# Two attentions on one core: sums over keys moved to TensorE, a normalization by 32x32 transposes, and a scheduler that keeps engines free for the next scores

## The chip, the cores and the metric

One core of one Trainium2 chip. The time is device microseconds (us) of one execution. ScalarE is called ACT in the profile, TensorE PE (its weight loads PEld), VectorE DVE, GpSimd POOL. A matmul here always needs its stationary operand loaded first; "step" means the time from the start of one instruction to the start of the next on the same engine.

## The reference, cut to what matters

Two attentions over 2048 positions and 448 channels, 16 heads of 28, their results side by side.

```python
# A: 16 query heads share one key and one value head
scores = einsum("bhqd,bkd->bhqk", q, k) * Dh ** -0.5      # 16 x 2048 x 2048
o = einsum("bhqk,bkd->bhqd", softmax(scores), v)          # then @ wo
# B: every query sees W = 8 keys, at distances 0, 2, ..., 14
logits = einsum("bhsd,bhswd->bhsw", q, k[idx]) * scale    # masked before position 0
o = einsum("bhsw,bhswd->bhsd", softmax(logits), v[idx])   # then @ wo
```

A's 67 million exponentials are the bulk. B is small, and is worked off beside A.

## The kernel before

The program is straight-line code, ordered by a planner inside the kernel. Every operation is added with an engine, a planned duration in us and a priority. The planner runs the engines forward in its own time, takes on each the best ready operation, and so fixes the order of each engine's instructions. Only the order reaches the chip: there each instruction starts when its engine is free and its semaphores have come.

```python
class Sched:
    LAT = 0.13                        # planned semaphore latency
    FULL = {2: 1500.0, 3: 1200.0}     # below this activity, scores use the full array height
    ...
def t_mm(n):                          # planned duration of one matmul of n columns
    return 0.02 + 0.42e-3 * max(n, 100)          # 0.235 us for 512
```

A's loop: the scores lie in PSUM in two slots of three and two banks. TensorE fills a slot, ScalarE takes the exponential of the whole slot (1536 or 1024 columns) and frees it. In 60 of the 410 rounds the third score goes to VectorE instead, which reads it (`d_x`) and approximates the exponential; its slot is free only after both reads. Scores need 28 rows of the array. They are issued as three matmuls beside each other in 32-row tiles (planned 0.32), or, when TensorE has been little active, one after the other at full height.

```python
def qk(e):                                    # scores of one slot
    for i, (sc, t, tb, j) in enumerate(us):
        if box[0].full:                       # full height, zero-padded keys
            e.matmul(g.bank(b0 + i), g.kz[:, j, ...], g.qT[:, sc % 2, t, :], ...)
        else:                                 # 32-row tile at row 32 j
            e.matmul(g.bank(b0 + i), g.kT[32*j:32*j+32, ...], g.qT[32*j:32*j+32, ...],
                     tile_position=(32 * j, 0))
```

B's eight products per block (`prod2`) are added in pairs on VectorE (`padd`), and TensorE sums the four that remain while it transposes. A's result for four heads and 512 queries lies in one PSUM bank, each head in 32 partitions, the sum of the exponentials in row 28. It is normalized in six stages over four engines:

```python
# a_quad_end: PV -> PV_sb copy (VectorE; ScalarE for the last one)
#   -> 4 fp32 matmuls with sel4 pick the sums -> reciprocal (VectorE)
#   -> rrep broadcast (GpSimd) -> 4 matmuls with ident -> product oTn (VectorE)
```

The softmax here doesn't subtract the row's maximum and nothing guards it: scores larger than these inputs give would overflow.

## Time and profile before

| | |
|---|---|
| time, median of 3 | 479.02 us (478.52 to 479.02) |
| profiled run | 476.5 us from the first to the last instruction, clock 1.000 |
| exponentials | 410 on ScalarE, from 12.67 to 467.75 us |
| last A output issued, last B output issued | 473.54, 474.06 us |

The prediction below shows most of the profile's lines. Some more: two groups by shape (busy us and mean ns of one, then idle time of the engine before them and what ended it), and the end of the timeline (columns: start in us, length in us, engine, line, operation, what it writes and reads, count).

```profile
L748 PEld LDWEIGHTS ps<-qT,kz 128*128 128x128 bf16 x305 | 21.1, 101 | 34.7 <-ACT expT L766 25.9 <-issue 0.7 <-ACT gcol L671 0.2
L823 DVE TENSOR_SCALAR d_x<-ps 128x512 f32<-128x512 f32 x60 | 41.4, 689 | 11.3 <-PE ps L750 7.4 <-PE ps L748 2.6
```

**How lateness is counted.** Throughout, the "late sum" adds, over all pairs of exponentials with no other ScalarE instruction between, the step minus 1.330 us after a 1536-column one and minus 0.904 us after a 1024-column one. Before it is 18.4 us. Steps at least 0.06 us late are sorted by the scores that the second exponential waited for: full-height scores, row-tiled scores behind a busy TensorE, and slots that VectorE's `d_x` read released late.

### The profile page before, as it was taken

The numbers are of one execution on the slowest core, as the hardware profiler recorded it, in microseconds if no ns is written. First come the engines' busy times: TensorE is split into PE (matmuls) and PEld (weight loads), VectorE is DVE, ScalarE is ACT, GpSimd is POOL, SyncE is SP. The second block draws the span as 40 slices with busy tenths as digits, with TensorE's granted clock in tenths as the row PEclk, the third lists the DMA queues.
The fourth block names the chain that finished last, engine by engine and source line by source line (L and its number), as shares of the span: only waits on it lengthen the run. The fifth ranks groups of instructions, "written<-read, shape, count | busy, mean of one in ns | idle before, by whom it ended". The sixth has DMA issues, their size and how long they took to land.

```text
span 476.5 us, 8559 instructions
## 1 busy us (share of the span) xinstructions
PE 451.4 (95%) x3605; PEld 178.3 (37%) x3605; DVE 375.6 (79%) x614; ACT 454.6 (95%) x431; POOL 29.4 (6%) x45
## 2 busy tenths in 40 slices
PE   8999999999999999999999999989999999989896
PEld 3443333434333424333434333333343343433332
DVE  4446878988878886889868887989868988896963
ACT  3899999999999999999999999999999999999993
POOL 8100010000000000000000010010001000010100
PEclk9999999999999999999999999999999999999999
DMA  9780211020200320002200330020200330220001
GB/s 195 147 216 1 89 30 58 11 78 12 87 11 30 111 83 12 11 19 79 78 11 10 107 107 11 10 78 12 87 12 21 107 106 12 88 88 11 0 11 48
DMA packets 41717, 27.32 MB, mean 57 GB/s; under 512 B 17090, under 2 KB 41520, under 8 KB 41680
## 3 DMA queue, kind: packets, MB, share of 16 engines
q1 hardware_dynamic: 39600, 25.25, 18.4%
q10 hardware_dynamic: 1776, 0.81, 0.7%
q0 software_dynamic: 304, 0.73, 0.6%
q8 instruction: 28, 0.46, 0.4%
q14 instruction: 9, 0.07, 0.1%
HBM read 17.60 MB, written 5.52 MB: 49 GB/s over the span
## 4 chain that ended last, share of the span: by engine, by line
ACT 65%; PE 31%; SPq 1%; DMA 1%; DVE 1%; issue 0%; DVEq 0%
ACT expT L766 64%; PE ps L750 7%; PE ps L924 6%; PE ps L790 5%; PE ps L748 4%; PE ps L852 2%; PE ps L696 2%; PE ps L940 1%; SPq L560 1%; DMA xT_A<-in_A_x_dram 1%; PE ps L883 1%; PE ps L1038 1%; PE ps L660 1%; PE ps L392 1%; ACT e_t L1001 0%
## 5 line engine op out<-in xcount | busy, mean ns | idle before, releaser
L766 ACT ACTIVATE expT<-ps 128x1024 bf16<-128x1024 f32 (+1 forms) x410 | 446.1, 1196 | 7.2 <-PE ps L750 4.5
L750 PE MATMUL ps<-qT,kT 32*128 32x512 bf16 x719 | 107.9, 384 | 8.8 <-ACT expT L766 5.9
L748 PE MATMUL ps<-qT,kz 128*128 128x512 bf16 x305 | 88.1, 382 | 9.6 <-ACT expT L766 7.5
L790 PE MATMUL ps<-expT,v_aug 128*32 128x512 bf16 x964 | 95.7, 389 | 0.4
L750 PEld LDWEIGHTS ps<-qT,kT 32*128 32x128 bf16 x719 | 26.5, 90 | 73.8 <-ACT expT L766 52.3
L823 DVE TENSOR_SCALAR d_x<-ps 128x512 f32<-128x512 f32 x60 | 41.4, 689 | 11.3 <-PE ps L750 7.4
L966 DVE TENSOR_TENSOR stage<-qTB,kTB 112x1024 bf16<-112x1024 bf16 x64 | 42.8, 682 | 9.1 <-PE ps L975 9.0
L790 PEld LDWEIGHTS ps<-expT,v_aug 128*32 128x32 bf16 x964 | 24.4, 92 | 66.3 <-issue 62.3
L924 PE MATMUL ps<-xT_B,wqkv 128*112 128x512 bf16 (+1 forms) x128 | 44.6, 407 | 0.0
L860 POOL COPY rrep<-rden 128x512 bf16<-128x512 bf16 x15 | 16.8, 1122 | 393.8 <-DVE rden L858 393.8
L1020 DVE TENSOR_TENSOR prod<-Vsh,a_n 128x896 bf16<-128x896 bf16 x64 | 38.4, 624 | 1.3 <-PE ps L1031 1.3
L830 DVE SCALAR_TENSOR_TENSOR d_u<-d_x 128x1024 f32<-128x1024 uint16 x30 | 36.5, 1217 | 0.1
L834 DVE SCALAR_TENSOR_TENSOR dexp<-d_u,d_x 128x1024 int16<-128x1024 f32 x30 | 36.4, 1214 | 0.1
L832 DVE SCALAR_TENSOR_TENSOR d_u<-d_u,d_x 128x1024 f32<-128x1024 f32 x30 | 36.3, 1211 | 0.1
L748 PEld LDWEIGHTS ps<-qT,kz 128*128 128x128 bf16 x305 | 21.1, 101 | 34.7 <-ACT expT L766 25.9
L1031 PE MATMUL ps<-ident,prod 128*112 128x128 bf16 x256 | 25.6, 226 | 0.0
L975 PEld LDWEIGHTS ps<-ones,stage 112*128 112x128 bf16 x512 | 20.5, 96 | 12.7 <-issue 7.0
L975 PE MATMUL ps<-ones,stage 112*128 112x4 bf16 x512 | 24.3, 167 | 0.0
L1031 PEld LDWEIGHTS ps<-ident,prod 128*112 128x112 bf16 x256 | 19.3, 129 | 12.1 <-issue 8.6
L924 PEld LDWEIGHTS ps<-xT_B,wqkv 128*112 128x112 bf16 (+1 forms) x128 | 14.1, 126 | 20.7 <-issue 17.4
L852 PEld LDWEIGHTS ps<-sel,PV_sb 128*128 128x128 f32 x128 | 18.9, 190 | 5.7 <-issue 4.1
L696 PE MATMUL ps<-xT_A,wq 128*128 128x512 bf16 x64 | 20.5, 384 | 0.5 <-DVE v_aug L675 0.3
(107 smaller groups left out, 383.0 us busy)
## 6 DMA issues: line engine op xcount, KB each, us to landing
Vsh<-v_scratch SPq DMA_DIRECT2D x16, 896.0 KB, 4.6
v_scratch<-Vst SPq DMA_DIRECT2D x16, 112.0 KB, 1.7
out_dram<-outB SPq DMA_DIRECT2D x16, 112.0 KB, 1.7
out_dram<-outA SPq DMA_DIRECT2D x14, 112.0 KB, 1.7
wqkv<-in_B_wqkv_dram SPq DMA_DIRECT2D x1, 672.0 KB, 5.0
stage<-in_A_x_dram ACTq DMA_DIRECT2D x1, 448.0 KB, 3.4
wo_B<-in_B_wo_dram SPq DMA_DIRECT2D x4, 98.0 KB
wo<-in_A_wo_dram SPq DMA_DIRECT2D x4, 98.0 KB
```

Source lines behind the costliest of these rows:

```text
L748: r = e.matmul(g.bank(b0 + i), g.kz[:, j, 128 * tb:128 * tb + 128], g.qT[:, sc % 2, t, :], start=True, stop=True)
L750: r = e.matmul(g.bank(b0 + i), g.kT[32 * j:32 * j + 32, 128 * tb:128 * tb + 128], g.qT[32 * j:32 * j + 32, sc % 2, t, :], start=True, stop ...
L766: x = a("act", t_exp(w), lambda e, b0=b0, w=w, n=n: e.activation(g.expT[:, n % ERING, 0:w], g.ps[:, 512 * b0:512 * b0 + w], ACT.Exp, scale ...
L790: x = e.matmul(g.bank(PVBANK, p0=32 * j, p1=32 * j + 32), g.v_aug[:, w, tb, :], src, start=first, stop=last, tile_position=(0, 32 * j))
L823: a("dve", t_dve_ps(512), lambda e: e.tensor_scalar(out=xx[:, 512 * h:512 * h + 512], in0=g.bank(bank), scalar1=-128.0 * A2, scalar2=128.0 ...
L830: a("dve", t_dve_1x(1024), lambda e: e.scalar_tensor_tensor(out=u, in0=lo, scalar=EP * F, in1=lo, op0=ALU.add, op1=ALU.mult), R=di, W=["d_ ...
L834: a("dve", t_dve_1x(1024), lambda e: e.scalar_tensor_tensor(out=out, in0=v, scalar=EL / F ** 3, in1=xx, op0=ALU.mult, op1=ALU.subtract), R ...
L924: a("pe", t_mm(512), lambda e, u=u, t=t, kt=kt, w=w: e.matmul(g.bank(u.bank, p1=KC), g.wqkv[64 * (kt // 3):, kt, w * D + KC * t:w * D + KC ...
L966: op = a("dve", t_dve_2x(1024), lambda e, t=t, qv=qv, kv=kv: e.tensor_tensor(out=g.prodT[0:KC, t, :, :], in0=qv, in1=kv, op=ALU.mult), R=R ...
L975: r = e.matmul(g.bank(u.bank, 128).rearrange("p (h w) -> p h w", w=WIN)[:, 4 * t:4 * t + 4, w], g.prodT[0:KC, t, w, :], g.ones4[:, :], sta ...
L1020: a("dve", t_dve_2x(2 * D), lambda e, qr=qr, Vv=Vv, av=av: e.tensor_tensor(out=g.prod2[:, 2 * qr:2 * qr + 2, :].rearrange("p w (d h) -> p ...
L1031: a("pe", 0.09, lambda e, u=u, t=t, w=w: e.matmul(g.bank(u.bank, 128, 128 * t, p1=KC), g.padd[:, w, KC * t:KC * t + KC], g.ident[:, :], st ...
```

## The change

Its intent: take B's pair additions off VectorE, replace the six-stage normalization by four VectorE instructions, and let the planner refuse work on TensorE and VectorE that would run into the next scores or the next `d_x` read. Offloaded scores now join the ordinary PV groups (PV: the product of the exponentials with the values) two passes over both slots later (`LATE`). B is released earlier. The core of the diff:

```diff
+            limit = None
+            H = tE["act"] + sum(o.dur for (_, o) in cand["act"] if o.ring)   # when ScalarE runs dry
+            if e == "dve":
+                ...
+                    limit = max(r1, H + (0.9 if n < 1 else 0) - self.QKT - 2 * self.LAT - 0.69)
+            if e == "pe":
+                ...
+                    limit = max(rq, H - self.QKT - self.LAT)
...
+                    if limit is not None and not o.ring and T + o.dur > limit + self.EPS:
+                        nxt = limit if nxt is None else min(nxt, max(limit, T + 0.02))
+                        continue
...
-                elif (o.full and area(T) < self.FULL[o.full]
+                elif (o.full and area(T) < (self.FULL[o.full] if T + 0.03 + 0.216 * o.full + self.LAT <= H + self.EPS else self.LOW)
```
```diff
     # a_quad_end
-    PV_sb copy, 4 matmuls with sel4, reciprocal, rrep on GpSimd, 4 matmuls with ident, product   # (abridged)
+            a("dve", t_dve_ps(w), lambda e, cs=cs: e.transpose(out=g.PV_T[:, t % 2, cs], in_=g.bank(PVBANK)[:, cs]), ...)
+            a("dve", 0.25, lambda e, pt=pt, bs=bs: e.reciprocal(out=g.rden[:, t % 2, bs], in_=pt[:, bs, DH]), ...)
+            a("dve", t_dve_1x(w), ... product with rden broadcast over 32, to oN ...)
+            a("dve", 0.12 + 1.04e-3 * w, ... e.transpose(out=g.oTn[:, t, cs], in_=oN) ...)
     # b_out
-        for hf in range(2): padd = prod2[hf] + prod2[hf + 2]      # VectorE (abridged)
-            for w in range(4): matmul(padd[:, w], ident)
+            for w in range(WIN): matmul(prod2[:, w], ident)       # WIN = 8
-    B0 = 32.0
-    BSTEP = 24.5
+    B0 = 30.0
+    BSTEP = 23.6
```

## The prediction

> **What bounds the kernel now.** I read four views in this order: the page's busy table and chain, the groups by shape, the instructions at ScalarE's late starts, and the end of the timeline.
>
> ```profile
> PE   451.4 (95%) x3605; PEld 178.3 (37%) x3605; DVE 375.6 (79%) x614; ACT 454.6 (95%) x431; POOL 29.4 (6%) x45
> PEclk9999999999999999999999999999999999999999
> ACT 65%; PE 31%; SPq 1%; DMA 1%; DVE 1%; issue 0%; DVEq 0%
> L766 ACT ACTIVATE expT<-ps 128x1024 bf16<-128x1024 f32 x264 | 264.9, 1047 | 2.7 <-PE ps L750 2.0 <-PE ps L748 0.4
> L766 ACT ACTIVATE expT<-ps 128x1536 bf16<-128x1536 f32 x145 | 213.3, 1471 | 4.5 <-PE ps L750 2.5 <-PE ps L748 1.4
> ```
>
> ScalarE and TensorE both show 95%. ScalarE's is real work: 410 exponentials in one row from 12.67 to about 467.7 us. TensorE's contains filler (L369, L392) and full-height scores (L748) that are issued to keep its clock up. The 31% of PE in the chain is not 31% of the end: the chain goes back through the producer of each exponential, and as long as that producer ended in time it cost nothing. So the question is when it was late. The idle column before the exponentials says 7.2 us, but it understates the loss. Consecutive activations overlap by some 0.1 us, so a start that is 0.1 us late shows no idle time. I therefore took, from the trace's instruction starts, the step from each exponential to the next one. Undelayed (the 5th percentile) it is 1.330 us after a 1536-wide one and 0.904 us after a 1024-wide one. The sum of what lies above these is 18.4 us: 1.0 us after the 1536-wide and 17.4 us after the 1024-wide. The asymmetry has a reason: after a 1024-wide exponential the next slot's three score matmuls have only 0.9 us to be refilled.
>
> Of the 18.4 us, 15.8 us are in 75 steps of 60 ns or more. I sorted these by the score group in front:
> - 38 steps, 7.0 us: three full-height scores. They need 0.844 to 0.858 us from the first to the exponential, and at best start 0.055 us after the slot is released, together 0.91 us: more than 0.904 less the overlap, so even on time they cost some 0.11 to 0.2 us each.
> - 26 steps, 6.8 us: row-tiled scores (0.437 us) that found TensorE occupied. In front of them stood mostly B's projections L924 (3.8 us) and the fp32 sums L852 (1.8 us).
> - 11 steps, 2.0 us: the slot was released late by VectorE's read of an offloaded score (d_x).
>
> ```profile
> 54.52 1.13 PE L924 MATMUL ps<-xT_B,wqkv 128*112 128x512 bf16 x3
> 55.58 0.39 PE L750 MATMUL ps<-qT,kT 32*128 32x512 bf16 x3
> 56.02 2.02 ACT L766 ACTIVATE expT<-ps 128x1024 bf16<-128x1024 f32 x2 [0.58 <-PE ps L750]
> ...
> 467.99 0.40 PE L790 MATMUL ps<-expT,v_aug 128*32 128x512 bf16 x4
> 468.44 0.60 ACT L844 ACTIVATE PV_sb<-ps 128x512 f32<-128x512 f32 x1 [0.69 <-PE ps L790]
> 469.09 1.05 PE L852 MATMUL ps<-sel,PV_sb 128*128 128x4 f32 x8
> 470.19 0.26 DVE L858 RECIPROCAL rden<-ps 128x16 bf16<-128x16 f32 x1 [7.86 <-PE ps L852]
> 470.48 0.43 DVE L860 COPY rrep<-rden 128x512 bf16<-128x512 bf16 x1
> 470.96 0.40 PE L866 MATMUL ps<-ident,rrep 128*128 128x128 bf16 x4 [0.36 <-DVE rrep L860]
> 471.42 0.74 DVE L871 TENSOR_TENSOR oTn<-PV_sb,ps 128x256 bf16<-128x256 f32 x2
> ```
>
> Above the dots is one late start: the slot was free at about 54.5 us, but three projections were in front, and ScalarE idled 0.58 us. Below them is the exposed end: from the last PV (about 468.4) to the second half of oTn (472.16) 3.77 us, 3.4 us to the first half.
>
> **What the Trainium skill says.** (1) "VectorE: DVE Perf Modes", The three transpose paths: VectorE transposes in 32x32 blocks only. That suits here, since PV holds each head in one block of 32 partitions. It gives 311 ns for 128 columns of bf16; no transpose is in this trace. (2) The same page, The perf-mode tier table: a PSUM or fp32 operand holds tensor_tensor at one element a cycle. The trace agrees: 512 columns from PSUM take 0.68 to 0.69 us, 128x896 in bf16 only 0.62. (3) "TensorE: Matmul & The Clock Gate", Part 1: the clock halves when the array is too little active over windows of some 3.4 us. The trace shows 1.00 in every stretch, so nothing here tells how far activity may fall. (4) "ScalarE: Activation LUTs", What ACT_TABLE_LOAD costs: 186 ns + 0.833 ns an element, back to back some 93 ns less, so 946 ns at 1024. The trace's undelayed 904 ns is shorter and is what I use.
>
> **The change part by part.**
>
> B's sums. 32 additions on VectorE go (32 x 0.657, 20.4 us busy). TensorE sums eight products where it summed four: 256 more matmuls at 87 ns (mean step from one L1031 to the next instruction) = +22.3 us.
>
> Normalization. TensorE loses 128 fp32 instructions at a step of 118 ns (15.2 us) and 64 broadcasts at 121 ns (7.7 us), together -22.9 us. TensorE is thus unchanged in sum (-0.6), but what it gains is in pieces of 0.09 us that fit between scores, and what it loses stood in front of late scores. VectorE loses the PV copies (10.2), reciprocals (4.1), products (10.3 + 0.7) and one rrep copy (0.4): -25.7 us. It gains for each of 16 quads: transpose of 512 fp32 columns from PSUM, estimated 0.69 as other PSUM reads of that width; reciprocal 0.25; product in fp32 0.68; transpose in bf16, estimated 0.65 at one element a cycle; 2.27 us, +36.3 us in all. VectorE in sum: -20.4 - 25.7 + 36.3 = -9.8 us, to about 366. GpSimd loses 16.8 us, which nobody waited long for (oTn's waits of 4.3 us are VectorE's own). None of this is on ScalarE, and the offload pattern stays (the new entry applies to a quad number that doesn't occur), so the 410 exponentials with their 436.7 us of undelayed steps and other ScalarE work stay. Busy sums therefore win nothing inside the loop.
>
> The scheduler's holding. It is the part that counts. It refuses work on TensorE or VectorE that would run past the latest harmless start of the next scores or d_x read, and takes full-height scores only where they fit before ScalarE runs dry or where activity is below a lower limit. What it can win is bounded by the 15.8 us. By kind:
> - Full-height triples: its check doesn't quite admit them behind a 1024-wide exponential, so they remain only in sparse stretches. I take 7.0 to 2.0: 5.0 us.
> - TensorE occupied: the kernel's own durations are short of the trace for projections (0.235 us planned, 315 ns measured step for L924, 272 for L940), so three of them in a gap run 0.24 us past the plan. I take 6.8 to 2.6: 4.2 us.
> - d_x late: 2.0 to 0.8: 1.2 us.
> Sum 10.4 us. I leave the other 2.6 us of jitter.
>
> The end. PV to oTn becomes eight VectorE instructions on halves of 256: transposes 2 x 0.41, reciprocals 2 x 0.2, products 2 x 0.43, transposes 2 x 0.39 (estimated from the 0.413 us of a 256-wide product), 2.86 us, first half done at 2.47, plus 0.1 of start: against 3.44 and 3.77 some 0.85 us gained. B's last block now also lies earlier (its releases start at 30 and step 23.6, so the last comes at 384 instead of 399.5 us), so VectorE should be free there.
>
> Sum: 10.4 + 0.85 = 11.2 us, from 479.0 to **467.8 us** (-2.3%).
>
> **The rivals.**
> - Held engines fall behind: holding costs capacity. Speaking for it: TensorE at 95%, B's block 15 still unfinished at 470 us. Against: over 12.7 to 467.7 us VectorE is busy 366 of 455, and filler plus the dispensable part of full-height scores on TensorE is some 40 us. If true, B's remainder or late PV (its bank is single) gives back 4 to 8 us: 472 to 476.
> - The clock drops, because fewer full-height scores and fillers are issued: nothing in this trace shows the limit. One throttled stretch of 20 us would cost more than the gain: 480 or more.
> - The change works as planned and nearly all late starts go: 15.8 + 0.9, some 462 us. Against: the projections' durations.
> - Only the operations matter, not the holding: then -0.85 us at the end and perhaps 2 us from L852 no longer in the way, 476 us.
>
> **Range and chances.** Eight in ten: 463.0 to 473.5 us. The low side is limited by 459.8 us, which removing all 18.4 us and 0.85 us would give. The 2% line is 469.4 us, just above my number, so faster 0.62, within 2% 0.35, slower 0.03 (the clock).
>
> **What would show it.** ScalarE's exponentials still 410 with the same undelayed steps; the sum of late steps near 8 us; the full-height score row well below 305; VectorE near 366 us busy; transposes of 0.6 to 0.7 us; TensorE clock 1.00; the interval from last PV to oTn near 2.9 us. I am wrong if ScalarE shows new waits on PV or expT, if the clock falls below 1.00, if B's work runs after the last exponential, or if the transposes from PSUM take much over 0.7 us.

## More of the kernel before

Projections come in four parts over the 448 channels. The fourth has only 64 rows of its own and uses a 64-row tile:

```python
for kt in range(4):                           # B's queries and keys; V and A's queries likewise
    a("pe", t_mm(512), lambda e: e.matmul(
        g.bank(u.bank, p1=KC), g.wqkv[64 * (kt // 3):, kt, ...],
        g.xT_B[64 * (kt // 3):, kt, 512 * c:512 * c + 512], start=kt == 0, stop=kt == 3,
        tile_position=(64 * (kt // 3), 0)), ...)
```

```profile
472.99 0.86 SPq L895 DMA_DIRECT2D out_dram<-outA  x2
474.06 0.33 SPq L1043 DMA_DIRECT2D out_dram<-outB  x1
```

B's last block already leaves after A's last one, by half a microsecond.

## The result, and the profile after

The changed kernel is correct. Its four runs took 474.87, 475.08, 475.72 and, at a lower clock, 495.45 us; the kernel before 478.77 us (median of 4). A ratio here is the mean time of one kernel's fast runs over that of the other's fast runs of the same rounds, so not quite the ratio of the medians: 0.9926, 95% interval 0.9907 to 0.9946. The gain is 0.7%, where 2.3% was predicted, and 475 us lies above the predicted range. The slow run is left out; its cause is not settled (see the end of the experiments).

The page after, its busy times, TensorE's clock and the chain:

```profile
PE 436.5 (92%) x3629; PEld 173.3 (37%) x3684; DVE 365.2 (77%) x600; ACT 451.8 (96%) x430; POOL 12.5 (3%) x30
PEclk9999999999999999999999999999999999999999
ACT 70%; PE 26%; DVE 1%; DMA 1%; issue 1%; ACTq 0%
```

VectorE is at 365 us as predicted (366), TensorE's clock is full, ScalarE's share rose by one point. The groups by shape (busy us and mean ns of one, then idle time of the engine before them and what ended it):

```profile
L785 ACT ACTIVATE expT<-ps 128x1024 bf16<-128x1024 f32 x264 | 266.3, 1065 | 2.9 <-PE ps L768 2.0 <-PE ps L766 0.7
L785 ACT ACTIVATE expT<-ps 128x1536 bf16<-128x1536 f32 x145 | 215.7, 1487 | 3.0 <-PE ps L768 2.5
L766 PE MATMUL ps<-qT,kz 128*128 128x512 bf16 x189 | 58.6, 382 | 12.1 <-ACT expT L785 8.5 <-issue 1.5 <-DVE PV_T L874 0.5
L846 DVE TENSOR_SCALAR d_x<-ps 128x512 f32<-128x512 f32 x60 | 41.5, 691 | 45.2 <-PE ps L768 39.2 <-PE ps L766 5.1
L874 DVE STREAM_TRANSPOSE PV_T<-ps 128x512 f32<-128x512 f32 x15 | 10.6, 710 | 1.6 <-PE ps L813 1.5
L882 DVE STREAM_TRANSPOSE oTn<-oN 128x512 bf16<-128x512 bf16 x15 | 10.5, 701 | 0.1
```

The same 410 exponentials. Full-height scores fell from 305 to 224 matmuls. The weight loads tell the number, since this trace lacks 35 of the matmuls' records (x189):

```profile
L766 PEld LDWEIGHTS ps<-qT,kz 128*128 128x128 bf16 x224 | 14.3, 97 | 27.0 <-ACT expT L785 22.2 <-issue 0.5
```

In the plan these are 41 triples before and 14 after; the 91 pairs stay. VectorE now stands idle 45.2 us in front of its `d_x` reads (11.3 before): the holding does hold. The transposes take 0.71 and 0.70 us. All of this is as predicted. The late sum is not: 15.4 us, where 18.4 - 10.4 = 8 was expected. A late start of the changed kernel, in the timeline:

```profile
206.76 1.02 ACT L785 ACTIVATE expT<-ps 128x1024 bf16<-128x1024 f32 x1
206.91 0.85 PE L936 MATMUL ps<-xT_B,wqkv 128*112 128x512 bf16 x3
207.69 0.39 PE L768 MATMUL ps<-qT,kT 32*128 32x512 bf16 x3
208.13 1.45 ACT L785 ACTIVATE expT<-ps 128x1536 bf16<-128x1536 f32 x1 [0.36 <-PE ps L768]
```

The slot was free when the previous exponential had ended (206.76 plus about 0.1). Three projections still went first. The planner took them for 3 x 0.235 = 0.705 us; from the first one's start to the scores they took 207.69 - 206.91 = 0.78, and they had begun late themselves. ScalarE idled 0.36 us. In the planner's own times this exponential follows the one before without a gap. This is the picture that holding should have removed.

The end of the changed kernel:

```profile
464.41 0.40 PE L813 MATMUL ps<-expT,v_aug 128*32 128x512 bf16 x4
464.86 0.78 DVE L874 STREAM_TRANSPOSE PV_T<-ps 128x256 f32<-128x256 f32 x2 [2.64 <-PE ps L813]
465.57 0.31 DVE L877 RECIPROCAL rden<-PV_T 128x8 f32<-128x8 f32 x2
465.80 0.72 DVE L879 TENSOR_TENSOR oN<-PV_T,rden 128x256 bf16<-128x256 f32 x2
466.44 0.77 DVE L882 STREAM_TRANSPOSE oTn<-oN 128x256 bf16<-128x256 bf16 x2
...
467.98 0.86 SPq L907 DMA_DIRECT2D out_dram<-outA  x2
468.10 0.85 ACTq L907 DMA_DIRECT2D out_dram<-outA  x2
468.46 0.69 DVE L1041 CAST oT<-ps 112x512 bf16<-112x512 f32 x1
...
470.83 0.33 SPq L1050 DMA_DIRECT2D out_dram<-outB  x1
```

The new normalization is quick: from the last exponential's end (464.17) to the last of `oTn` (467.20) it takes 3.03 us, where the old one took 472.16 - 467.75 = 4.41. A's last output is issued at 468.53. But B's last block is issued at 470.83, and the program ends with it. From the last exponential to the end the changed kernel needs 472.97 - 464.17 = 8.80 us, the one before 8.79. So of the 3.6 us between the two profiles, 0.36 come from an earlier first exponential (12.31 for 12.67), 3.2 from the loop, and none from the end.

### The profile page after: what moved, and what is told of

Read it like the earlier page. It is cut to its first block, busy times and chain, and to the rows that moved or that the text cites. A ratio compares the mean times of both kernels' runs of the same rounds, so it can differ in the third digit from the quotient of the medians.

```text
span 473.0 us, 8630 instructions
## 1 busy us (share of the span) xinstructions
PE 436.5 (92%) x3629; PEld 173.3 (37%) x3684; DVE 365.2 (77%) x600; ACT 451.8 (96%) x430; POOL 12.5 (3%) x30
## 3 DMA queue, kind: packets, MB, share of 16 engines
q1 hardware_dynamic: 39600, 25.25, 18.4%
## 4 chain that ended last, share of the span: by engine, by line
ACT 70%; PE 26%; DVE 1%; DMA 1%; issue 1%; ACTq 0%
ACT expT L785 69%; PE ps L768 6%; PE ps L936 6%; PE ps L813 4%; PE ps L714 2%; PE ps L766 2%; PE ps L952 2%; DMA d_x<-in_A_wq_dram 1%; PE ps L643 1%; ACT e_t L1013 1%; PE ps L895 1%; PE ps L678 1%; PE ps L413 1%; PE ps L1045 1%; PE ps L728 0%
## 5 line engine op out<-in xcount | busy, mean ns | idle before, releaser
L768 PE MATMUL ps<-qT,kT 32*128 32x512 bf16 x800 | 118.7, 384 | 14.5 <-ACT expT L785 11.2
L813 PE MATMUL ps<-expT,v_aug 128*32 128x512 bf16 x964 | 99.3, 389 | 0.1
L846 DVE TENSOR_SCALAR d_x<-ps 128x512 f32<-128x512 f32 x60 | 41.5, 691 | 45.2 <-PE ps L768 39.2
L766 PE MATMUL ps<-qT,kz 128*128 128x512 bf16 x189 | 58.6, 382 | 12.1 <-ACT expT L785 8.5
L768 PEld LDWEIGHTS ps<-qT,kT 32*128 32x128 bf16 x800 | 29.2, 90 | 80.8 <-ACT expT L785 51.8
L1038 PE MATMUL ps<-ident,prod 128*112 128x128 bf16 x512 | 48.5, 226 | 0.2 <-issue 0.2
L1038 PEld LDWEIGHTS ps<-ident,prod 128*112 128x112 bf16 x512 | 36.7, 129 | 21.8 <-issue 17.9
L766 PEld LDWEIGHTS ps<-qT,kz 128*128 128x128 bf16 x224 | 14.3, 97 | 27.0 <-ACT expT L785 22.2
L936 PEld LDWEIGHTS ps<-xT_B,wqkv 128*112 128x112 bf16 (+1 forms) x128 | 14.2, 127 | 22.5 <-issue 18.3
L714 PE MATMUL ps<-xT_A,wq 128*128 128x512 bf16 (+1 forms) x60 | 19.9, 385 | 1.3 <-DVE v_aug L693 0.6
L952 PE MATMUL ps<-wqv,xT_B 128*128 128x448 bf16 x64 | 19.4, 358 | 0.0
L1045 PE MATMUL ps<-wo_B,oT 112*128 112x448 bf16 x64 | 18.1, 356 | 0.8 <-DVE oT L1041 0.8
```

The lines of the kernel that those rows point to most:

```text
L766: r = e.matmul(g.bank(b0 + i), g.kz[:, j, 128 * tb:128 * tb + 128], g.qT[:, sc % 2, t, :], start=True, stop=True)
L768: r = e.matmul(g.bank(b0 + i), g.kT[32 * j:32 * j + 32, 128 * tb:128 * tb + 128], g.qT[32 * j:32 * j + 32, sc % 2, t, :], start=True, stop ...
L813: x = e.matmul(g.bank(PVBANK, p0=32 * j, p1=32 * j + 32), g.v_aug[:, w, tb, :], src, start=first, stop=last, tile_position=(0, 32 * j))
L846: o = a("dve", t_dve_ps(512), lambda e: e.tensor_scalar(out=xx[:, 512 * h:512 * h + 512], in0=g.bank(bank), scalar1=-128.0 * A2, scalar2=1 ...
L936: a("pe", t_mm(512), lambda e, u=u, t=t, kt=kt, w=w: e.matmul(g.bank(u.bank, p1=KC), g.wqkv[64 * (kt // 3):, kt, w * D + KC * t:w * D + KC ...
L1038: a("pe", 0.09, lambda e, u=u, t=t, w=w: e.matmul(g.bank(u.bank, 128, 128 * t, p1=KC), g.prod2[:, w, KC * t:KC * t + KC], g.ident[:, :], s ...
```

## The experiments

Theory D: the late starts that the planner foresees with its own durations can be planned away; the rest arises because TensorE's projections take longer than planned, and holding cannot see it. Rivals are stated with each run. All runs are correct, with five rounds and the kernel before beside them. Numbers from profiles are of fast runs.

| run | fast median, us | ratio | first exp. | last exp. ends | to the end | late sum | full height | TensorE busy | d_x late |
|---|---|---|---|---|---|---|---|---|---|
| before | 478.8 to 479.2 | 1 | 12.67 | 467.75 | 8.79 | 18.4 | 7.0 | 6.8 | 2.0 |
| changed | 475.08 | 0.9926 | 12.31 | 464.17 | 8.80 | 15.4 | 2.8 | 8.9 | 1.5 |
| 1 new operations, no holding | 477.17 | 0.9954 | 12.68 | 469.07 | 6.99 | 19.6 | 8.5 | 7.1 | 2.4 |
| 2 holding, old operations | 481.27 | 1.0041 | 12.85 | 463.80 | 14.69 | 14.2 | 1.9 | 8.6 | 1.8 |
| 3 changed + durations | 468.03 | 0.9760 | 14.35 | 459.24 | 7.66 | 8.6 | 1.1 | 4.7 | 1.1 |
| 4 changed, other release | 474.92 | 0.9904 | 12.99 | 465.54 | 7.53 | 16.0 | 1.5 | 11.0 | 1.6 |
| 5 holding + durations, old operations | 475.96 | 0.9924 | 13.56 | 458.25 | 16.77 | 8.2 | 2.1 | 3.8 | 0.5 |
| 6 before + durations | 473.30 | 0.9873 | 13.11 | 461.47 | 9.68 | 11.5 | 6.0 | 2.8 | 1.0 |
| 7 run 3 improved | 466.91 | 0.9745 | 12.64 | 457.13 | 7.76 | 8.0 | 0.8 | 4.0 | 1.5 |
| 8 planner knows tile shapes | 464.57 | 0.9693 | 13.10 | 455.72 | 7.00 | 6.3 | 1.8 | 1.8 | 0.9 |
| 9 changed, full-row projections | 470.62 | 0.9812 | 12.88 | 459.80 | 8.80 | 10.4 | 3.0 | 4.7 | 0.9 |

The last three columns count steps of 0.06 us or more, so they add up to less than the late sum. Runs 10 and 11 are missing because their profiles fell in slow runs. The ratios of runs 1 to 4 and 9 to 11 lie some 0.1% low, since the fast runs of the kernel before beside them include a few at a lower clock (480.6 and 483.5 us; 485.6 us); the medians hardly feel these.

**Run 1: the new operations alone.**

```diff
-                if r1 is not None:
+                if False and r1 is not None:            # VectorE not held
-                if rq is not None and T > 14:
+                if False and rq is not None and T > 14: # TensorE not held
-    ... area(T) < (self.FULL[o.full] if T + 0.03 + ... <= H + self.EPS else self.LOW)
+    ... area(T) < self.FULL[o.full]
-                    if T > 14 and area(T) > self.LOW:
+                    if False and T > 14 and area(T) > self.LOW:
```

> The changed kernel with the scheduler's holding switched off (new operations and releases stay). Theory D (holding removes only the late starts that the scheduler's own durations foresee; the rest comes from TensorE instructions that take longer than planned): the late steps of ScalarE return to 16 to 19 us and full-height triples to about 40; B's last block ends before A's, so the gain at the end shows; 476 to 478.5 us. Rival O (the new operations carry the whole gain): 474.5 to 475.7 us with late steps near 15 us.

477.17 us, late sum 19.6, full-height scores back at 8.5 us: as D expects (the sum a little above its range). In this profile the granted clock was 0.50 from 351.3 to 358.1 us, and four late steps there make 2.3 us of the sum; without them it is 17.3, inside the range. B's last block left at 450.59 us, and from the last exponential to the end it is 6.99 us. So the new normalization is worth 8.79 - 6.99 = 1.8 us at the end when B is out of the way. Rival O, that the operations carry the whole gain with a late sum near 15, fails on the late sum. In time it fails by less: the clock of these runs was between 0.991 and 1.000 and the times between 476.1 and 479.0, the intervals of the two ratios overlap, and the three runs at a clock of 0.998 or more took 476.1 to 476.3 us, where the changed kernel took 474.9 to 475.7. So the operations alone bring over half of the gain, most of it at the end; what holding wins in the loop, B's late end largely takes back.

**Run 2: the holding alone**, added to the kernel before with no new operation.

> The kernel before with the holding alone (old sums, old normalization, old releases). Theory D: late steps fall from 18.4 to 13 to 16 us, triples to about 10; 474.5 to 477 us, or a little more where B's last block becomes the end. Rival O: 478 to 480 us.

A miss: 481.27 us, slower than before. The loop did what D said: late sum 14.2, last exponential 4 us earlier. But B fell behind. The end of its timeline:

```profile
461.64 2.16 ACT L787 ACTIVATE expT<-ps 128x1536 bf16<-128x1536 f32 x2
464.30 0.60 ACT L867 ACTIVATE PV_sb<-ps 128x512 f32<-128x512 f32 x1 [0.50 <-PE ps L812]
472.20 0.99 PE L1054 MATMUL ps<-ident,prod 128*112 128x128 bf16 x14 [0.22 <-DVE prod L1047]
476.34 0.33 SPq L1066 DMA_DIRECT2D out_dram<-outB  x1
```

B's last block is summed at 472 and issued at 476.34 us, 12.5 us after the last exponential. Held engines don't lose the work that they refuse; they do it later, and here after the end of A. I had named this as a rival, and put it aside on busy sums. A rival that no run tests: B kept its old release here. The planner, run once more off the chip with run 7's release (34 and 22.0), ends B at 457.8 us where it planned 464.6 for this run, so part of the loss may belong to the release and not to the holding.

**Run 3: right durations.** The planned durations of the projections and of the output products are set to the trace's steps. B is released 2 us earlier, so that the planner ends B in time.

```diff
-                    a("pe", t_mm(512), ... B's q and k
+                    a("pe", 0.26 + 0.05 * (kt > 1) + 0.04 * (kt > 2), ...
-                a("pe", t_mm(512), ... A's q           -> 0.225 + 0.09 * (kt > 1)
-            a("pe", t_mm(512), ... A's q, fifth part   -> 0.31
-            a("pe", t_mm(D), ... B's v                 -> 0.2 + 0.09 * (kt > 1)
-            a("pe", t_mm(D), ... B's and A's output    -> 0.19 + 0.09 * (last part)
-    B0 = 30.0
+    B0 = 28.0
```

> The changed kernel with the planned durations of the projections and output products set to the steps that the trace shows (0.26 to 0.35 us instead of 0.235), and B released 2 us earlier so that its last block is planned to end as in the fourth run. Theory D: late steps in front of row-tiled scores fall from 8.9 to under 5 us, all late steps from 15.4 to under 11; 468 to 471.5 us. Rival C (TensorE has no room, whoever plans): late steps 14 to 16 us or B's end later; 474.5 us or more.

468.03 us, 2.4% below the kernel before, inside the range of D. Late steps behind a busy TensorE fell from 8.9 to 4.7 us, the late sum to 8.6. No instruction became faster: only the order differs, and with it how many scores take the full height and how much filler is issued. Rival C (TensorE has no room) fails.

**Run 4: the control.** Changed kernel, old durations, only B's release moved (32 and 23.0). The planner promises the same end as in run 3.

> Control for the third: the changed kernel with its old planned durations and only another release of B (32 and 23.0), for which the scheduler plans the same end as in the third run. Theory D: the plan is no better kept than in the changed kernel, late steps 13 to 16 us, 473.5 to 475.5 us. Rival P (the changed kernel merely has an unlucky placement of B, and any shorter plan comes true): 470 to 472 us.

474.92 us, late sum 16.0, 11.0 of it behind a busy TensorE. An equally good plan with wrong durations is not kept. Rival P (unlucky placement) fails. The 6.9 us between runs 3 and 4 are what the right durations are worth at equal planned ends.

**Run 5: holding and durations on the old operations** (run 2 plus the durations, with the first block's Q left as it was).

> The second run (kernel before with the holding alone) plus the corrected durations. Theory D with B's backlog (holding alone failed because it defers B, whose last block then ends the program): late steps fall from 14.5 to under 10 us, the last exponential ends at 458 to 461 us, but B's last block still ends some 10 us after it, so 473 to 478 us. Rival S (old operations cost nothing, only the durations were wrong): 468 to 470 us as in the third run.

475.96 us, inside D's range. The last exponential ends at 458.25 us, 9.5 us earlier than before, but 16.8 us pass from there to the end: B again. Run 7, whose loop ends at 457.13 us, has the new operations and needs 7.76 us there, 9 less. Not all of this is shown to be the operations': run 7 also releases B's last block at 364 us instead of 399.5, and this run's last 7.8 us had a granted clock of 0.50. Run off the chip with run 7's release and the old operations, the planner ends B no earlier (474.1 us; 466.6 for this run), but a plan is not a run. From first to last exponential runs 3 and 5 take nearly the same time (444.89 and 444.69 us), so the new operations matter by letting B keep pace, and not in the loop.

**Run 6: durations without holding**, on the kernel before.

> The kernel before with the corrected durations alone, no holding. Theory D (the durations matter only because holding acts on them): late steps stay at 16 to 19 us, 477 to 480 us. Rival G (right durations help any schedule of this kernel): 472 to 475 us.

A miss of theory D as I had put it: 473.30 us, 1.3% faster, more than the whole change. Rival G was right. Late steps behind a busy TensorE fell from 6.8 to 2.8 us without any holding. The reason is in how the planner works: as long as the next scores are not ready in its own time, it starts other work. With durations that are too short, its clock reaches that moment after more projections than the chip can do by then, and on the chip the order is fixed. Full-height scores stay at 6.0 us, since only the changed kernel's fit check removes them. So D has to be stated more widely: wrong durations spoil the order of any such schedule; holding is not needed for them to matter.

**Run 7: run 3 improved.** The first block's Q keeps its planned durations (in run 3 they had moved instructions that wait for loads in front of the first scores, and the first exponential came at 14.35 us), `LATE = 3`, B released at 34 and 22.0.

> The third run improved: the first block's Q keeps its old planned durations (the third run started its exponentials at 14.35 instead of 12.3 us), offloaded probabilities enter PV three rounds later instead of two, B released at 34 and 22.0. Theory D: first exponential at 12.3 to 12.9 us, late steps 6 to 9 us, 464.5 to 467.5 us. If the start of the third run was chance of the loads, 466.5 to 468.5 us.

466.91 us, first exponential at 12.64: as expected.

**Run 8: the planner is told about tile shapes.** Instead of fixed longer durations, each TensorE operation gets a shape, and 0.095 us are added whenever the shape changes.

```diff
+    SW = 0.095
+            sw = lambda o: self.SW if e == "pe" and T > 14 and shape and shape != o.cfg else 0.0
-                    if limit is not None and not o.ring and T + o.dur > limit + self.EPS:
+                    if limit is not None and not o.ring and T + o.dur + sw(o) > limit - (self.SW if e == "pe" and o.cfg else 0) + self.EPS:
+                o.dur += sw(o)
 # B's q, k: 0.26; A's q: 0.22; 448 columns: 0.193; fourth part: its own shape; full-height scores +0.05
 # B's logits 0.115 instead of 0.2, its sums 0.06 instead of 0.09
 # LATE = 3, B0 = 24, BSTEP = 21
```

> Instead of fixed longer durations the planner adds 0.095 us wherever the next TensorE instruction uses another tile shape, and 0.26 us for a 112-column projection; planned full-height scores 0.05 us longer; B released at 24 and 21.0, offloaded probabilities three rounds later. If the change of tile shape is the mechanism of the drift, late steps are at most those of the seventh run (5 to 9 us) and the time 463.5 to 467.5 us; if it is not, they return to over 11 us and 470 us or more.

464.57 us, 3.1% below the kernel before and 2.2% below the changed one (464.57 / 475.08 = 0.978): the best version measured. Late steps behind a busy TensorE are down to 1.8 us. Its exponentials:

```profile
L792 ACT ACTIVATE expT<-ps 128x1024 bf16<-128x1024 f32 x264 | 278.5, 1164 | 0.0
L792 ACT ACTIVATE expT<-ps 128x1536 bf16<-128x1536 f32 x145 | 229.6, 1583 | 1.9 <-PE ps L774 1.6 <-PE ps L772 0.2
```

The idle time in front of them is 1.9 us, where the changed kernel had 5.9. (The records are longer, 1164 for 1065 ns, because each overlaps the one before by more; the steps are not.) What the charge for shapes is worth by itself is not shown, since the edit also corrects the planned durations of B's logits and sums. Part of the step from run 7 to run 8 may also be B's release, which was moved: here B is done at 450.98 us and the end takes 7.00 us, 0.76 less than in run 7.

**Run 9: the mechanism by itself.** The changed kernel with exactly its order of instructions; the fourth part of each projection uses all 128 rows, with zero weights in the other 64, in place of a 64-row tile. This makes it more arithmetic, not less.

```diff
-   g.wqkv[64 * (kt // 3):, kt, ...], g.xT_B[64 * (kt // 3):, kt, ...], ..., tile_position=(64 * (kt // 3), 0))
+   g.wqkv[:, kt, ...], g.xT_B[:, kt, ...], ...)          # likewise B's v and A's q
+   memset(g.wqkv[0:64, 3, :], 0.0); memset(g.wqv[0:64, 3, :], 0.0)     # GpSimd, at the start
```

> The changed kernel with the same order of instructions, but the fourth part of each projection, which used 64 of the 128 rows as a tile of its own, uses all 128 with zero weights in the other 64. No instruction is added on TensorE and none moved. If a change of tile shape costs the unplanned 0.095 us (theory D's mechanism), the step from the third to the fourth part falls from 0.31 to about 0.22 us (0.26 for the 112-column ones), late steps in front of row-tiled scores fall from 8.9 to 5 to 7.5 us, and the time to 472 to 474 us. If each new stationary operand costs it whatever its shape, nothing changes: 475 to 475.7 us.

470.62 us, 1% below the changed kernel, a little better than the expected range; late steps behind a busy TensorE 4.7 us. The same group of four parts in the changed kernel and in this run, from the timeline of TensorE:

```profile
65.03 1.21 PE L936 MATMUL ps<-xT_B,wqkv 128*112 128x512 bf16 x4
```
```profile
64.51 1.07 PE L938 MATMUL ps<-xT_B,wqkv 128*112 128x512 bf16 x4
```

1.21 against 1.07 us for one projection, and that counts only the changes inside the group. In the traces' instruction starts, where nothing stands between them, the step from the third to the fourth part of B's projections is 0.31 us (11 of 19) or 0.35 (8) with the 64-row tile, and 0.22 (11) or 0.26 (8) without; in A's Q it is 0.31 to 0.32 with it and 0.22 to 0.23 without. The weight loads of the same groups show where the 0.09 us lie:

```profile
65.03 0.39 PEld L936 LDWEIGHTS ps<-xT_B,wqkv 128*112 128x112 bf16 x3 [0.23 <-DVE dexp L858]
65.81 0.12 PEld L936 LDWEIGHTS ps<-xT_B,wqkv 64*112 64x112 bf16 x1 [0.39 <-issue]
```
```profile
64.51 0.61 PEld L938 LDWEIGHTS ps<-xT_B,wqkv 128*112 128x112 bf16 x4 [0.23 <-issue]
```

In the changed kernel the fourth part's load starts 1 to 2 ns before its own matmul in 31 of 32 projections. In run 9 it starts 213 to 225 ns before it in 20 of 32, beside the matmul before (in the other 12 scores or PV, of another shape, come directly before). Each part loads another stationary operand in both cases, so it is not the new weights but the new tile shape that costs: the load is no longer hidden. Nor is it the small tile: a 128-row part that follows a 64-row one steps at 0.35 us as well (7 of 7 in the changed kernel).

**Run 10: full rows and the shape-aware planner together** (run 8 plus run 9's edit, B released at 24 and 22.5).

> The eighth run (planner that charges a change of tile shape) with the same full-row projections, B released at 24 and 22.5, which plans the same end as the eighth run's. TensorE saves up to 64 changes of shape, some 6 us, but the planner already knew of them, so theory D expects no more than the late steps of the eighth run, 5 to 7 us, and 463.5 to 465.5 us. If TensorE's time were the limit (rival C), 461 to 463 us.

464.53 us fast median, ratio 0.9685: the same as run 8. A planner that knows the cost had, it seems, already placed it where it does no harm. Its profile fell in a slow run and is not used.

**Run 11: B released at 33**, one number of the changed kernel.

> The changed kernel with one number changed: B released at 33 instead of 30 us. The planner's last exponential stays within 0.01 us, but its last block of B is planned 10 us before A's end instead of 2 us after it. If B's last block is what hides the new normalization's gain at the end, the time from the last exponential to the end falls from 8.8 to about 7.0 us and the whole to 472.5 to 474.5 us; if that gain does not exist, it stays at 8.8 and 475 us.

Its fast runs have a median of 474.51 us, ratio 0.9903: half a microsecond below the changed kernel, short of the 472.5 to 474.5 expected, at the edge. The profile fell in a slow run, so its loop cannot be used. Its end can, with care: the clock was low only from 17.2 to 54.7 us and in the last 1.3 us, B's last block was issued 9 us before A's (474.55 against 483.58), and from the last exponential to the end it is 7.00 us, as expected. That B's last block hides the gain at the end thus rests on runs 1 and 8, with 6.99 and 7.00 us, and this profile agrees. Where the fast runs lost most of these 1.8 us again stays open.

**What stays open.** Some runs of all kinds were slow: the changed kernel once (495.45 us, mean clock 0.945), runs 10 and 11 once, the kernel before at 480.6 to 487.6 us with clocks of 0.996 to 0.975. The slow profile of run 11 shows where (run 10's shows the same from 14.5 to 35.0 us):

```profile
PEclk9755799999999999999999999999999999999999
```

The clock falls in the second to fifth slice (about 12 us each), the start of the loop, and is full after. The kernel before shows it as well, so I don't lay it to the change; whether the change makes it more frequent, four runs cannot say.

## Why the prediction was wrong

The steps of the prediction, in its own order:

- **ScalarE's work and the undelayed steps stay**: right (410; 0.904 and 1.330 us).
- **VectorE to about 366**: right, 365.2. Its parts: transposes 0.71 and 0.70 us for estimated 0.69 and 0.65, reciprocal 0.24, product 0.68.
- **Full-height triples, 7.0 to 2.0**: right, 2.0, and 0.8 in one full-height pair.
- **d_x late, 2.0 to 0.8**: 1.5; 0.7 us short.
- **TensorE occupied, 6.8 to 2.6**: this is the step that failed. It became 8.9, which is 6.3 of the 7.3 us between the predicted and the measured time. The prediction itself had the cause in hand: "three of them in a gap run 0.24 us past the plan". It then took 4.2 us off all the same. It should have asked, of the late steps before, which the planner had foreseen. (Of its split of the 6.8 us, the 3.8 behind L924 come out again; directly behind L852 a recount finds 0.9, not 1.8.)

The planner's own start times answer that. They come from the kernel, which computes them while it builds its program; an exponential counts as foreseen late when the planner itself leaves more than 0.02 us between it and the one before. Lateness on the chip in steps of 0.06 us or more not foreseen, and lateness in foreseen ones:

| | foreseen | not foreseen |
|---|---|---|
| before | 9.1 | 6.7 |
| changed | 3.5 | 9.7 |
| run 1, no holding | 10.4 | 7.6 |
| run 2, holding alone | 2.8 | 9.5 |
| run 6, before + durations | 8.1 | 1.7 |
| run 3, changed + durations | 2.1 | 4.8 |
| run 8, shapes planned | 2.3 | 2.2 |

Holding removed 5.6 of the 9.1 us that could be planned away (with the new operations and no holding, run 1, it was 10.4; with holding 3.5). It added 3.0 us to what could not. With nothing but the holding changed it is 2.8 (before to run 2) or, leaving run 1's stretch at half the clock out, 3.4 (6.3 to 9.7). The likely reason, read from the code and not measured: holding lets work fill a gap right up to the last allowed moment, with 0.03 us of grace, so that an overrun of a projection meets ScalarE. Correct durations do the reverse. Of the predicted 10.4 us in the loop, 3.0 came (18.4 to 15.4); full-height scores gave 4.2 (7.0 to 2.8), d_x 0.5 and the small steps 0.4, and scores behind a busy TensorE took 2.1 back (6.8 to 8.9).

A cause of the overruns is the tile shape: matmuls of one shape in a row step at 216 ns for 512 columns, but a 64-row tile that follows a 128-row one takes 310 ns, and 235 were planned. The fourth part's shape alone makes 4.2 of the 8.9 us (run 9, with the order kept). Run 8 brings them to 1.8. How the rest divides between other changes of shape (to the scores and to PV) and the 112-column parts, whose steps are in part 260 ns within one shape, was not separated.

- **The end, 0.85 us**: the mechanism was right and undersized: 1.38 us to `oTn`, 1.8 us in all. But nothing of it was seen, because B's last block became the end by 2.3 us (470.83 against 468.53). The prediction's sentence "B's last block now also lies earlier ... so VectorE should be free there" took the release time for the finishing time. Releases are earlier, but with the same releases and operations B's first and last blocks left at 134 and 471 us in the changed kernel and at 118 and 451 us in run 1: held engines let B fall behind. The planner's own times said so before any run: in its plan for the changed kernel B's output lands 2.2 us after A's last. B's work after the last exponential was also one of the prediction's signs of being wrong.
- **The rival "held engines fall behind"** was thus partly true, as it stood in the list: not through PV or its bank, but through B's remainder. Run 2 shows it at full size, 12.5 us after the last exponential. Its 472 to 476 us contain the result partly by luck: B's end hid 1.8 us, and the larger loss, scores behind a busy TensorE, is none of its reasons. **The rival that only the operations matter** (476 us) comes close in time, and its late starts do not. **The rival of the clock** is not supported by fast runs.

## What to carry to other kernels

In a statically ordered program the planned durations are part of the program: measure the step of each instruction in its context, not the length of it alone, and charge what stands between unlike neighbours. Before planning waits away, split them into those that the plan foresees and those that it doesn't; a tighter plan removes the first kind and sharpens the second. And work refused in one place comes back in another: look at what ends last after the change, here the small attention that nobody was waiting for.

## What the Trainium skill lacked or had wrong

- "TensorE: Matmul & The Clock Gate", Part 2, gives a step of N/2.4 + 2.5 ns for matmuls in a row. That holds here within one tile shape (216 ns at 512 columns, 189 at 448, with some steps of 226 and 200; none shows the 131 ns that the same part gives for 512 columns with a weight load each) and not where the next one uses another: 309 to 354 ns for a 64-row tile after a 128-row one, 285 at 448 columns. Part 3 of the same page says that weight loads overlap running matmuls only when the row groups differ; with equal row groups most loads of run 9's fourth parts were hidden (they start 213 to 225 ns before their matmul), and with a 64-row tile after a 128-row one they were not (1 to 2 ns).
- The same page ties fast weight loads to 128 columns. The runs agree (LDWEIGHTS of 112 columns 128 ns, of 128 columns 97 ns); that steps of 112-column parts are in part longer too (260 ns in all 21 first steps of B's projections, mostly 216 in the second) is not said.
- "TensorEngine Tiling (Array Packing)", Key Properties, says that changing the tiling mode drains TensorE, which the prediction overlooked. It gives no time, and no other page does: here a change costs about 0.095 us.
- "VectorE: DVE Perf Modes", The three transpose paths, has one duration for VectorE, 128 columns of bf16. The runs add 0.71 us for 512 fp32 columns read from PSUM, 0.70 for 512 of bf16 from SBUF, 0.43 and 0.42 us for 256.
- "ScalarE: Activation LUTs", What ACT_TABLE_LOAD costs: 186 ns + 0.833 ns an element less 93 ns of overlap gives 946 and 1373 ns at 1024 and 1536 columns, without naming PSUM; the undelayed steps here, read from PSUM, are 904 and 1330.
